# Output stores of four steps begun by ScalarE, in ScalarE's own DMA queue, instead of SyncE

## The chip, the cores and the metric

One core of a Trainium2 chip runs the kernel. The metric is the device time in microseconds (us) of one launch. The engines are named as in the profile: PE (TensorE, matmul), PEld (its weight loads), DVE (VectorE), ACT (ScalarE), POOL (GpSimd) and SP (SyncE). SP computes nothing here; it begins transfers. "ACTq" and "SPq" are the sequencers of ACT and SP: rows with that name issue transfers or wait.

## The reference

For each of 33280 tokens of 192 numbers, a convolution over the token and the six before it, with softmax weights that depend on token and head, and then a layer of 1024 hidden units:

```python
def _attn_ref(x, weight_gen):            # x (8, 4160, 192), weight_gen (8, 4160, 8, 7)
    w = softmax(weight_gen, axis=-1)     # over the 7 taps
    out = np.einsum('bshk,bskhg->bshg', w, x_unf)   # x_unf: the token and 6 before it
    return out.reshape(B, S, D)

def _moe_ref(x, w_in, w_out, g_ln):      # w_in (192, 1024), w_out (1024, 192)
    h = x @ w_in
    solu = h * softmax(h)
    ln = (solu - mean(solu)) / sqrt(var(solu) + 1e-6) * g_ln
    return ln @ w_out
```

## The kernel before

Each of the 128 partitions holds a run of 260 consecutive tokens. Step t (0 to 259) works on one token of each partition, so on 128 tokens. Inputs arrive in chunks of 16 steps (`load_x` in four parts, L87; `load_w`, L93). POOL multiplies taps and inputs for four steps at a time (L180) and adds part of the products (L195). From there a step runs like this:

- PE turns the step's inputs over (L477, two steps at a time). ACT copies the high half of them in 16 bits (`xhi`, L487), DVE the rest (`xld`, L491), and SP swaps halves between partitions with two small transfers (`sw`, L497).
- `mm1` (L511, L516): PE's first product, 128 x 1024, into one of three buffers `h`.
- `max` on DVE (L528), `exp` on ACT (L534), `solu` on DVE (L542), `sq` on ACT (L548): the softmax, its product with h, and the sums. Each is followed by a short read of the sum it collected.
- `hi` on ACT (L555) and `lo` on DVE (L559) write the result as two 16-bit halves into `hl` (three buffers).
- `tr` (L567): SP begins a transposing transfer hl to `hlT` (six buffers). An ACT `hi` that finds no free `hl` buffer waits until an earlier transposing transfer has landed.
- `mm2` (L607): PE's second product, 24 matmuls into `po`. There is one buffer `po`, so mm2 of the next step waits until `out` has read it.
- `out` (L618): ACT scales po into the step's place in `ot`, a tile of four steps with two buffers.
- `od` (L622): after every fourth `out`, the store of `ot` to memory, 384 KB. There are 66: 64 of four steps, one of three, one of the last step.

Every four steps there are also six small operations on the statistics, three of them on ACT (L582; L586 and L588; L594), and every 16 steps some on the input's norm (L145, L156 to L169) and the taps (L115, L120).

Each engine works its instructions off in the order in which the program was written. That order comes from a planner (`plan`, `issue_order`) that plays the whole program through with a table of costs and prints one list; the functions below are called in that list's order, so the place of an instruction among those of its engine is its place in the list. In the planner, `od` is a step of SP. Transfers begun by SP or ACT use eight semaphores in turn, in the order of the list, whichever engine begins them. A transfer waits, on the engine that begins it, until the transfer eight before it has landed.

Of the kernel before, what the change touches and what calls it, by code (L numbers as in the profile page):

```python
# [26 lines left out]
def tile_kernel(ctx: ExitStack, tc: tile.TileContext, x, weight_gen, w_in, w_out, g_ln, out):  # L27
    nc = tc.nc
# [10 lines left out]
    TG = 4  # L39
# [19 lines left out]
    o_run = out.rearrange("(p t) d -> p t d", t=RUN)  # L59
# [372 lines left out]
    o_of = {}  # L432
# [186 lines left out]

    def store(t):  # L620
        t0 = RUN - 1 if t == RUN - 1 else t - t % TG
        nc.sync.dma_start(o_run[:, t0 : t + 1, :], o_of[t // TG][:, t0 % TG : t % TG + 1, :])  # L622

    def at(op, *args):
        return lambda t: op(t, *args)
# [4 lines left out]
    def at_chunk(op, *args):  # L630
# [4 lines left out]
        xhi=high_x, xld=low_x, mm1=first_product,  # L635
        max=maximum, exp=exponentials, solu=solu, sq=squares, hi=high_half, lo=low_half,
        tr=transpose_s, mm2=second_product, out=finish, od=store, lw=at_chunk(load_w),
    )
    for n in range(2):
# [69 lines left out]
    t0=132.6, t0_0=11.9, t0_4=-51.5, t1=101, t1_0=56.2, t1_4=-6.3, t2=148.6, t2_0=60.2, t2_4=246.7,  # L709
# [335 lines left out]
```

## Time and profile before

| | |
|---|---|
| three runs | 1245.5, 1243.78, 1245.46 us, median 1245.46 |
| the profiled execution | 1243.28 us, its span 1241.5 us |
| busy share of the span | PE 96%, DVE 93%, POOL 92%, ACT 91% |
| granted TensorE clock | 0.996 over the span |
| transfers | 219.18 MB, most of them in packets under 512 B |
| stores (L622) | 64 of 384.0 KB, one of 288.0 KB, one of 96.0 KB; 3.4 us from issue to landing (median) |

The span runs from the first to the last instruction of the program; the 1.8 us between it and the execution's time lie around the program. A busy share is an average over the whole span. A wait is told with the engine and line that waited, what it waited for, and then microseconds in total, how often, and the longest. Waits of sequencers (SPq, ACTq) are not part of an engine's idle time. A transfer's row on SPq or ACTq lasts as long as the sequencer is busy beginning it, not until the data has landed.

### The profile page before, as it was taken

What the parts mean: (1) busy time and instruction counts of PE and PEld (TensorE: products, weight loads), DVE (VectorE), ACT (ScalarE), POOL (GpSimd) and SP (SyncE); (2) the same over time, 40 slices, a digit from 0 to 9 for tenths busy, and PEclk for the clock granted to TensorE, in tenths of its full rate; (3) what the DMA queues carried; (4) which work ended last, traced back from release to release, by engine and by line L of the source; (5) the groups of instructions that cost most, each with busy time, mean ns of one, the idle gap of its engine ahead of it and who ended that gap; (6) DMA issues with size and microseconds to landing.
All of it is one profiled execution on the core that took longest, in us unless ns stands there. A gap on an engine that the chain in (4) does not pass through costs nothing. (4 is left out here: it accounts for less than half of the span.)

```text
span 1241.5 us, 27360 instructions
## 1 busy us (share of the span) xinstructions
PE 1188.7 (96%) x10296; PEld 818.6 (66%) x10296; DVE 1151.7 (93%) x1777; ACT 1127.1 (91%) x2286; POOL 1140.1 (92%) x235
## 2 busy tenths in 40 slices
PE   1799999999999999999999999999999999999998
PEld 1467666666666676666666666666666666666766
DVE  6778989999899999999999999999999999999994
ACT  5789999899999989899998999999898999988895
POOL 5999999999999999999999999999999999999500
PEclk9899999999999999999999999999999999999999
DMA  7579797888988889898978989898988979887685
GB/s 246 106 158 223 139 217 158 182 177 182 194 161 203 166 190 181 178 206 144 219 154 192 185 177 207 158 204 171 184 178 176 216 149 200 159 156 138 137 166 125
DMA packets 585491, 219.18 MB, mean 177 GB/s; under 512 B 548623, under 2 KB 566031, under 8 KB 585102
## 3 DMA queue, kind: packets, MB, share of 16 engines
q1 hardware_dynamic: 585056, 216.32, 84.2%
q8 instruction: 81, 1.33, 0.4%
q10 hardware_dynamic: 302, 1.11, 0.3%
q14 instruction: 52, 0.43, 0.1%
HBM read 45.60 MB, written 25.56 MB: 57 GB/s over the span
## 5 line engine op out<-in xcount | busy, mean ns | idle before, releaser
L180 POOL TENSOR_TENSOR pr<-xt,wt 128x5376 f32<-128x5376 f32 (+1 forms) x67 | 631.2, 9420 | 0.2
L607 PE MATMUL po<-w_hl,hlT 128*128 128x192 f16 x6168 | 551.1, 246 | 6.9 <-ACT ot L618 6.9
L607 PEld LDWEIGHTS <-hlT 128*128 128x128 f16 x6240 | 522.8, 98 | 52.6 <-issue 10.6
L195 POOL TENSOR_TENSOR pr<-pr 128x2304 f32<-128x2304 f32 (+1 forms) x122 | 449.5, 3684 | 7.4
L559 DVE SCALAR_TENSOR_TENSOR hl<-h,hl 128x1024 f16<-128x1024 f32 x260 | 316.4, 1221 | 41.6 <-ACT hl L555 24.7
L542 DVE SCALAR_TENSOR_TENSOR h<-h,row,e 128x1024 f32<-128x1024 f32 x260 | 333.0, 1282 | 15.5 <-ACT e L534 14.4
L528 DVE TENSOR_SCALAR_CACHE_REDUCE h<-h,row 128x1024 f32<-128x1024 f32 x260 | 334.3, 1286 | 5.9 <-PE h L516 5.3
L555 ACT ACTIVATE hl<-h 128x1024 f16<-128x1024 f32 x260 | 266.7, 1027 | 41.2 <-DVE h L542 20.9
L534 ACT ACTIVATE e<-h,stats 128x1024 f32<-128x1024 f32 x260 | 291.8, 1122 | 8.8 <-DVE h L528 7.8
L548 ACT ACTIVATE e<-h,stats 128x1024 f32<-128x1024 f32 x260 | 290.7, 1118 | 3.2 <-DVE hl L559 2.7
L516 PEld LDWEIGHTS <-xh 128*128 128x128 f16 x1560 | 131.5, 98 | 234.2 <-issue 111.8
L516 PE MATMUL h<-w_odd,xh 128*128 128x512 f16 x780 | 190.9, 381 | 0.0
L516 PE MATMUL h<-wa_hi,xh 128*128 128x512 f16 x520 | 178.2, 384 | 0.0
L618 ACT ACTIVATE ot<-po,stats 128x192 f32<-128x192 f32 x257 | 110.2, 429 | 29.9 <-PE po L607 29.8
L511 PE MATMUL h<-w_odd,turned 64*128 64x512 f16 x390 | 106.2, 379 | 5.8 <-DVE hl L559 4.6
L511 PE MATMUL h<-wb_hi,xh 64*128 64x512 f16 x260 | 99.5, 383 | 7.4 <-DVE hl L559 7.2
L511 PE MATMUL h<-w_odd,xh 64*128 64x512 f16 x390 | 106.3, 380 | 0.0
L477 PE MATMUL pa<-ident,pr 128*128 128x128 f32 x738 | 95.3, 277 | 7.7 <-POOL pr L180 3.9
L511 PE MATMUL h<-wb_hi,turned 64*128 64x512 f16 x260 | 99.6, 383 | 0.0
L477 PEld LDWEIGHTS pa<-ident,pr 128*128 128x128 f32 x738 | 86.2, 143 | 19.9 <-POOL pr L180 5.6
L516 PE MATMUL h<-wa_lo,xh 128*128 128x512 f16 x260 | 99.1, 381 | 0.0
L511 PEld LDWEIGHTS <-xh 64*128 64x128 f16 x780 | 53.7, 94 | 47.1 <-issue 22.6
(90 smaller groups left out, 995.8 us busy)
## 6 DMA issues: line engine op xcount, KB each, us to landing
out_dram<-ot SPq DMA_DIRECT2D x64, 384.0 KB, 3.4
xt<-in_x_dram SPq DMA_DIRECT2D x30, 576.0 KB, 4.7
xt<-in_x_dram SPq DMA_DIRECT2D x30, 480.0 KB, 4.3
turned<-xh SPq DMA_DIRECT2D x260, 32.0 KB, 2.2
wt<-in_weight_gen_dram SPq DMA_DIRECT2D x16, 448.0 KB, 5.4
hlT<-hl SPq DMA_TRANSPOSE x260, 4.9
xt<-in_x_dram SPq DMA_DIRECT2D x1, 1536.0 KB, 10.7
pr<-in_moe_w_out_dram SPq DMA_DIRECT2D x1, 1024.0 KB, 7.9
```

The costliest lines, as they stand in the source:

```text
L180: nc.gpsimd.tensor_tensor(out=window(pr, 0, [(ROW, K), (HG, n * H), (1, HG)]), in0=window(xt, t * D, [(D, K), (HG, n * H), (1, HG)]), in1= ...
L195: nc.gpsimd.tensor_tensor(out=b, in0=b, in1=a, op=ALU.add)
L477: nc.tensor.matmul(pa[:, k], source[:, first : first + P], ident, is_transpose=True, start=at == 0, stop=at == 3 * len(sources) - 1,)
L511: nc.tensor.matmul(h[:, fs], last[(f + odd) % 2][rows, low], rhs[rows], start=n == 0, stop=False)
L516: nc.tensor.matmul(h[:, fs], xh[:, 2 * odd, low], rhs[:, fs], start=False, stop=n == 2)
L528: nc.vector.tensor_scalar(h, h, row(t, BACK), 3.0e38, op0=ALU.mult, op1=ALU.min, accum_out=stat(t, NMAX))
L534: nc.scalar.activation(e, h_of[t], AF.Exp, bias=stat(t, NMAX), scale=-1.0, accum_out=stat(t, Z))
L542: nc.vector.scalar_tensor_tensor(out=h, in0=h, scalar=row(t, SCALE), in1=e, op0=ALU.mult, op1=ALU.mult, accum_out=stat(t, M))
L548: nc.scalar.activation(e_of.pop(t), h_of[t], AF.Square, bias=stat(t, M), scale=-float(FF), accum_out=stat(t, Q),)
L555: nc.scalar.activation(hl[:, 0, :], h_of[t], AF.Copy, scale=2.0**14)
L559: nc.vector.scalar_tensor_tensor(out=hl[:, 1, :], in0=h_of[t], scalar=2.0**14, in1=hl[:, 0, :], op0=ALU.mult, op1=ALU.subtract,)
L607: nc.tensor.matmul(po[:, :D], hlT[:, half * NJ + j, :], w2_hl[:, j, w, :], start=n == 0, stop=n == len(terms) - 1,)
```

## The change

The store calls ACT's queue instead of SP's. The planner still counts `od` as a step of SP, so the list, and with it the order of all other instructions on every engine, stays what it was: the 66 stores leave SP's stream and stand in ACT's, each at its place in the list.

```diff
     def store(t):
         t0 = RUN - 1 if t == RUN - 1 else t - t % TG
-        nc.sync.dma_start(o_run[:, t0 : t + 1, :], o_of[t // TG][:, t0 % TG : t % TG + 1, :])
+        nc.scalar.dma_start(o_run[:, t0 : t + 1, :], o_of[t // TG][:, t0 % TG : t % TG + 1, :])
```

The first place is the store of the tile ot_7630, at about 606 us of the profiled execution. In ACT's stream before, the fourth `out` of the tile (L618, ot_7630) is followed at once by `sq` (L548):

```order
L555 ACTIVATE hl_7807<-h_7684 128x1024
L534 ACTIVATE e_7811,stats_135<-h_7741,stats_135 128x1024
L618 ACTIVATE ot_7630<-po_7777,stats_135 128x192
L548 ACTIVATE e_7756,stats_135<-h_7684,stats_135 128x1024
L145 ACTIVATE junk_7860,squares_x_116<-xt_7636 128x768
L555 ACTIVATE hl_7862<-h_7741 128x1024
L618 ACTIVATE ot_7878<-po_7834,stats_135 128x192
```

And now, with the store right between them:

```order
L555 ACTIVATE hl_7807<-h_7684 128x1024
L534 ACTIVATE e_7811,stats_135<-h_7741,stats_135 128x1024
L618 ACTIVATE ot_7630<-po_7777,stats_135 128x192
L622 DMA out_0_dram<-ot_7630 128x768
L548 ACTIVATE e_7756,stats_135<-h_7684,stats_135 128x1024
L145 ACTIVATE junk_7860,squares_x_116<-xt_7636 128x768
L555 ACTIVATE hl_7862<-h_7741 128x1024
L618 ACTIVATE ot_7878<-po_7834,stats_135 128x192
```

The store now stands ahead of `sq` and of all that ACT does after it.

In SP's stream the same store stood before between parts of an input load and two transposing transfers:

```order
L497 DMA turned_7736<-xh_7698 64x256 x2
L87 DMA xt_7636<-in_x_dram 128x960
L567 DMA_TRANSPOSE hlT_7761<-hl_7739 128x16x128
L87 DMA xt_7636<-in_x_dram 128x1152
L622 DMA out_0_dram<-ot_7630 128x768
L567 DMA_TRANSPOSE hlT_7832<-hl_7807 128x16x128
L567 DMA_TRANSPOSE hlT_7883<-hl_7862 128x16x128
L497 DMA turned_7887<-xh_7804 64x256 x2
```

Now the transposing transfer of hl_7807 follows the load directly; the store no longer stands ahead of it, and nothing else moved.

The next store, of ot_7878 (about 625 us), stands in ACT's stream behind two small operations of the statistics:

```order
L618 ACTIVATE ot_7878<-po_8012,stats_135 128x192
L586 ACTIVATE stats_135<-stats_135 128x4
L588 ACTIVATE stats_135<-stats_135 128x4x2
L622 DMA out_0_dram<-ot_7878 128x768
L534 ACTIVATE e_8062,stats_135<-h_7991,stats_135 128x1024
L145 ACTIVATE junk_8094,squares_x_116<-xt_7636 128x768
```

Here `exp` (L534) is the next that comes behind the store. Of the 66 stores, ten follow their `out` directly; the others have one or two of ACT's instructions between: L586 and L588 (13), L487 (14), L582 (6), L162 and L163 (6), L594 (2), or a long one, L534, L548 or L555 (15).

## The prediction

> **What bounds the kernel now.** I read the page's busy shares first, then the busy time of each engine in stretches of the steady part, then the list of waits, then the timeline around two stores.
>
> ```profile
> span 1241.5 us, 27360 instructions
> PE 1188.7 (96%) x10296; PEld 818.6 (66%) x10296; DVE 1151.7 (93%) x1777; ACT 1127.1 (91%) x2286; POOL 1140.1 (92%) x235
> ...
> 500.00:700.00 200.00, 197.76 (x1729) 135.56 (x1727) 191.93 (x291) 186.79 (x376) 198.59 (x40) 1.00 0.90 186
> 700.00:900.00 200.00, 199.12 (x1734) 135.86 (x1732) 194.97 (x302) 188.51 (x383) 197.20 (x40) 1.00 0.89 181
> 900.00:1100.00 200.00, 199.00 (x1738) 136.61 (x1737) 193.21 (x297) 188.72 (x386) 197.63 (x40) 1.00 0.89 178
> ```
>
> The columns of the stretches are, after the length, the busy time of PE, PEld, DVE, ACT and POOL, then clock, DMA share and GB/s. PE is busy for 197.8 to 199.1 of 200 us at the full clock: in the steady part it sets the pace. Everything else is close behind. ACT has 11.3 to 13.2 us idle in 200, which at a store every 18.5 us (about 11 in 200) is 1.0 to 1.2 us for each store. What PE can still win there is 1 to 2 us in 200, some 10 us over the kernel; what it can lose has no such limit.
>
> ```profile
> ACT ot L618 <- PE po L607: 29.8, 28, 1.9
> PE po L607 <- ACT ot L618: 6.9, 13, 1.7
> PE h L511 <- DVE hl L559: 11.7, 13, 5.4
> ACT hl L555 <- DMA hlT<-hl: 6.1, 8, 1.7
> ```
>
> So PE waits for ACT in one place directly: mm2 cannot start before `out` has emptied the only `po`. And the whole cost of late transposing transfers to ACT is 6.1 us in 8 waits. mm2 does not appear in the list as waiting for one.
>
> SP, the queue that loses the stores, around 605 us:
>
> ```profile
> 599.98 0.58 SPq L87 DMA_DIRECT2D xt<-in_x_dram  x1
> 600.67 3.45 SPq L567 DMA_TRANSPOSE hlT<-hl  x1
> 604.22 1.17 SPq L497 DMA_DIRECT2D turned<-xh  x2
> 605.43 1.39 SPq L87 DMA_DIRECT2D xt<-in_x_dram  x1
> 606.94 3.33 SPq L567 DMA_TRANSPOSE hlT<-hl  x1
> 610.31 0.57 SPq L87 DMA_DIRECT2D xt<-in_x_dram  x1
> 610.98 0.38 SPq L622 DMA_DIRECT2D out_dram<-ot  x1
> 611.47 6.64 SPq L567 DMA_TRANSPOSE hlT<-hl  x2
> ...
> 618.19 1.02 ACT L555 ACTIVATE hl<-h 128x1024 f16<-128x1024 f32 x1 [0.98 <-DMA hlT<-hl]
> 619.25 1.22 DVE L559 SCALAR_TENSOR_TENSOR hl<-h,hl 128x1024 f16<-128x1024 f32 x1 [1.64 <-ACT hl L555]
> 620.67 2.14 PE L607 MATMUL po<-w_hl,hlT 128*128 128x192 f16 x24 [0.42 <-ACT ot L618]
> ```
>
> SP runs almost without a gap (about 0.1 us between transfers), most of it in transposing transfers of 2 to 3.5 us. The three last rows show where that lateness ends: `hi` waits 0.98 us, `lo` 1.64, and mm2 0.42.
>
> **What is removed from SP.** Each store and the gap behind it leave SP: 0.38 + 0.1 us here.
>
> ```profile
> L622 SPq DMA_DIRECT2D out_dram<-ot x66: 333/531/1332, 86.9 to 1238.5; - x66
> ```
>
> At the median it is 0.53 + 0.1, times 66 some 42 us of SP's time. It is worth only what late transfers cost. The bound is the 6.1 us of the third wait above passing whole into PE; in the example 0.42 of 0.98 us passed, which makes 2.6 us of 6.1; and the store's 0.48 us is half of the 0.98. I take a gain of 2 us, with 0 and 6.1 as the ends.
>
> **What is added to ACT.** Each store has three parts: the wait for its `out`, the time in which ACT's sequencer begins the transfer, and the return to the next instruction. The wait for the transfer eight places before costs nothing: seven before the store at 610.98 is the load at 599.98, so the eighth was begun over 5.9 us before this store's `out` is done (605.90 by the rows further down), and transposing transfers land 4.9 us after their issue at the median:
>
> ```profile
> DMA to landing us min/median/max: 4.2/4.9/8.4
> ```
>
> If a transfer is late there, all of ACT stands behind it; the cover is that distance.
>
> How long ACT's sequencer is held the trace does not show for this place. The nearest rows are SP's own stores and the first transfers of the kernel, where ACT and SP begin transfers side by side:
>
> ```profile
> 0.71 0.40 ACTq L205 DMA_DIRECT2D hlT<-in_moe_w_in_dram  x1
> 0.72 0.40 SPq L93 DMA_DIRECT2D wt<-in_weight_gen_dram  x1
> 1.15 1.16 ACTq L77 DMA_DIRECT2D xt<-in_x_dram  x2
> ...
> 294.54 2.37 SPq L567 DMA_TRANSPOSE hlT<-hl  x1
> 299.12 0.35 SPq L622 DMA_DIRECT2D out_dram<-ot  x1
> ...
> 624.05 1.93 SPq L567 DMA_TRANSPOSE hlT<-hl  x1
> 626.09 0.93 SPq L622 DMA_DIRECT2D out_dram<-ot  x1
> ```
>
> A store that finds SP idle takes 0.35 us (18 of them, 0.33 to 0.35). One right behind a transposing transfer takes longer: 31 of them, 0.53 to 1.33, median 0.89. So something that both use is still at work when SP's sequencer is through with the transposing transfer. ACT's transfers took 0.40 and 0.58 us beside SP's. For ACT's stores I take 0.54 where SP is not in a transposing transfer, and 0.89 where it is. Comparing the end of each of the 66 `out` rows with SP's rows, SP is in one at 37 of them, with 1.32 us still to go on average.
>
> Now what of this ACT feels. The two places:
>
> ```profile
> 605.47 0.43 ACT L618 ACTIVATE ot<-po,stats 128x192 f32<-128x192 f32 x1
> 606.32 1.12 ACT L548 ACTIVATE e<-h,stats 128x1024 f32<-128x1024 f32 x1 [0.42 <-DVE hl L559]
> 606.70 2.14 PE L607 MATMUL po<-w_hl,hlT 128*128 128x192 f16 x24
> 609.16 0.42 ACT L618 ACTIVATE ot<-po,stats 128x192 f32<-128x192 f32 x1
> 611.82 2.15 PE L607 MATMUL po<-w_hl,hlT 128*128 128x192 f16 x24
> ...
> 624.23 0.42 ACT L618 ACTIVATE ot<-po,stats 128x192 f32<-128x192 f32 x1
> 624.54 0.22 ACT L586 ACTIVATE stats<-stats 128x4 f32<-128x4 f32 x1
> 624.78 0.22 ACT L588 ACTIVATE stats<-stats 128x8 f32<-128x8 f32 x1
> 624.90 1.10 ACT L534 ACTIVATE e<-h,stats 128x1024 f32<-128x1024 f32 x1
> ```
>
> At the first, `out` ends at 605.90. ACT idled until 606.32 anyhow, so a store of 0.54 us with 0.12 for the two hand-overs (SP's gap between transfers) delays `sq` by 0.66 - 0.42 = 0.24 us. At the second, `out` ends at 624.65 and `exp` starts at 624.90: L586 and L588 cover 0.25, and 0.41 is left, provided that ACT's sequencer can begin a transfer while ACT still computes. Where a long instruction (1.1 us) stands between, nothing is left. Read so at all places, the delays are: ten directly behind `out`, 0.41 us each on average; 13 behind L586 and L588, 0.42; 6 behind L582, 0.56; 6 behind L162 and L163, 0.34; 14 behind L487, 0.18; 2 behind L594, 0.24; 15 behind a long one, 0. That is 4.1 + 5.5 + 3.4 + 2.0 + 2.5 + 0.5 = 18 us of ACT's time. With 0.35 us for every store it is 10, with 1.33 it is 58, and with the mixture I take (0.54 and 0.89) 28 us.
>
> Most of it is taken up before PE sees it. The next `out` after 605.90 ends at 609.58 and its mm2 starts at 611.82: 2.2 us of slack. After the `out` that ended at 605.90 itself it was 606.70 - 605.90 = 0.8. I carried each of the 66 delays down ACT's rows, took off the idle time in front of them, and charged PE with what is over the slack of the next `out`. An estimate, then: 0.1 us in all at 0.35 per store, 1.2 at 0.54, 6.7 for the mixture, 23 at 1.33 everywhere, 19 with 1.33 only beside transposing transfers. The same delay reaches DVE through `exp` and `hi`, and PE through the buffers `h`, where it waits 11.7 us now, one wait of 5.4 among them; I add 2 us for that (ends 0 and 6).
>
> The end of the kernel costs nothing either way: the last store is begun by whichever queue after the last `out`, and takes 0.33 us.
>
> **The sum**, against the profiled execution's 1243.28 us (1.8 of it around the span): + 6.7 + 2 - 2 = 1250.0. The median of the runs stands 2.2 us higher than that execution; I put the forecast between the two sums, at 1251. A measurement of this kernel tells about 0.2%, 2.5 us, from no change; this is 0.4%.
>
> **The rivals.**
> - The gain of SP is the larger part: ACT's stores take 0.35 to 0.40, as in its row at 0.71, and are covered, and SP's transposing transfers come earlier. ACT then costs 0.1 to 1 us and SP gives up to 6.1: 1239 to 1243 beside the median. For it: SP's rows stand end to end, and mm2 did wait 0.42 us at 620.67 after a chain that began there. Against it: only 8 waits for transposing transfers in the whole kernel. It decides if the gain exceeds 2.5 us, so if more than 40% of those 6.1 us were PE's. 22%.
> - Nothing that can be told from no change: 1.2 + 1 - 2, so within 2.5 us of 1245.5. It takes 0.54 us or less beside transposing transfers also. 23%.
> - ACT's queue cannot begin a transfer while SP's is beginning one. At the 37 places ACT's store then waits out SP's 1.32 us and starts after it. With 0.54 behind that, ACT feels 63 us and PE 40; with 0.89, 76 and 50, by the same carrying down. That is more than ACT's 1.0 to 1.2 us of idle per store at these places, and the time is 1283 to 1296. For it: the 0.93 us at 626.09 behind a transposing transfer. Against it: at 0.71 and 0.72 both sequencers are at it together and both take 0.40. 15%.
>
> The last of these is also the account of the Trainium skill. Its page Perfetto Trace Analysis, section DMA Instruction — HWDGE, says that a transfer's row holds a wait for a lock, that the descriptor generator is then locked for exclusive use, and that it is freed when all descriptors are made. By that rule the sum would be the one just given; the two rows of 0.40 us side by side do not agree with a lock over the whole row, but no transposing transfer is among them.
>
> **Chances and range.** The forecast, slower by 0.2 to 1.6%: 40%; with the queues that exclude each other, slower in all: 55%. Same 23%, faster 22%. The range leaves out the last rival (15%) and little at the low end: from 1239 (the whole gain) to 1275 (1.33 us at every store, 23 us, and 6 through DVE, on the median). The forecast's own range is 1248 to 1266.
>
> **What would show it.** Stores on ACTq: their duration, median near 0.54 and near 0.9 beside transposing transfers; over 1.5 there speaks for the last rival, 0.35 to 0.40 the covered case. ACT's idle before the instruction behind each store should be put down to the issue. PE's waits for L618 should grow from 6.9 us to about 13, and ACT's for hlT shrink from 6.1 to about 3. It would be wrong if ACT's sequencer cannot run ahead of the engine: then all 66 stores cost their full time, 35 us and more, whatever stands in front.

## The result, and the profile after

The kernel with ACT's stores took 1253.72 us (median of three runs), the one before 1245.32: 1.0066 of its time, 95% interval 1.0049 to 1.0082, or 8.2 us slower by that ratio. A second measurement gave 1254.0 us and 1.0063 (1.0045 to 1.0081). A fourth run of the first measurement, the profiled one, had a TensorE clock of 0.56 of full speed and took 2033.52 us, so it is not counted and the profile shown here is from the second measurement, at the same clock as that of before (0.997 and 0.996).

The page of the profile after, its first rows and the queues:

```profile
span 1251.7 us, 27310 instructions
PE 1191.7 (95%) x10296; PEld 818.8 (65%) x10296; DVE 1153.3 (92%) x1777; ACT 1132.2 (90%) x2286; POOL 1140.5 (91%) x235
...
q1 hardware_dynamic: 575552, 190.75, 78.6%
q10 hardware_dynamic: 9806, 26.67, 6.4%
```

The stores' 25.6 MB have left SP's queue (q1) for ACT's (q10). Every engine has as many instructions as before and is busy for 0.2 to 5.1 us more; every one also stands idle longer, PE by 7.2 us. The waits that answer to those shown before, and ACT's new ones:

```profile
ACT ot L618 <- PE po L607: 25.5, 27, 1.8
...
PE h L511 <- DVE hl L559: 15.8, 21, 5.4
...
PE po L607 <- ACT ot L618: 9.4, 14, 1.9
ACT hl L555 <- DMA hlT<-hl: 9.1, 9, 1.7
...
ACT e L534 <- issue: 2.3, 13, 0.2
...
ACT e L548 <- issue: 1.1, 6, 0.2
```

PE waits 4.1 us more for `lo` (11.7 before) and 2.5 more for `out` (6.9 before). ACT waits 3.0 us more for transposing transfers to free `hl` (6.1 before), where the forecast had 3 us less. The stores in the view of the tile ot, and then the landing of the transposing transfers (L567):

```profile
L622 ACTq DMA_DIRECT2D out_dram<-ot x66: 338/338/377, 82.4 to 1248.8; - x66
DMA to landing us min/median/max: 1.6/4.2/7.8
...
DMA to landing us min/median/max: 4.3/5.1/9.3
```

Each store holds ACT's sequencer for 0.338 us (median), at most 0.377; 39 of the 66 began while SP's sequencer was in a transposing transfer. The stores land after 4.2 us (3.4 before), the transposing transfers after 5.1 (4.9 before). At the places of the prediction, the stores of ot_7630 and ot_7878:

```profile
609.95 0.43 ACT L618 ACTIVATE ot<-po,stats 128x192 f32<-128x192 f32 x1
610.41 0.34 ACTq L622 DMA_DIRECT2D out_dram<-ot  x1
610.81 1.11 ACT L548 ACTIVATE e<-h,stats 128x1024 f32<-128x1024 f32 x1 [0.42 <-DVE hl L559]
...
627.39 0.43 ACT L618 ACTIVATE ot<-po,stats 128x192 f32<-128x192 f32 x1
627.70 0.22 ACT L586 ACTIVATE stats<-stats 128x4 f32<-128x4 f32 x1
627.95 0.22 ACT L588 ACTIVATE stats<-stats 128x8 f32<-128x8 f32 x1
627.96 0.35 ACTq L622 DMA_DIRECT2D out_dram<-ot  x1
628.36 1.11 ACT L534 ACTIVATE e<-h,stats 128x1024 f32<-128x1024 f32 x1 [0.19 <-issue]
```

The store begins 0.03 us after its `out`. At the first place the idle time of 0.42 us that was there before covers it whole. At the second it begins while L588 runs and leaves 0.19 us of idle ("issue": the engine waited for nothing else). So ACT's sequencer does begin transfers while ACT computes.

### The profile page after: what moved, and what is told of

It reads as the page before. It is cut to its first block, busy times and chain, and to the rows that moved or that the text cites. A ratio compares the mean times of both kernels' runs of the same rounds, so it can differ in the third digit from the quotient of the medians.

```text
span 2031.7 us, 27310 instructions
## 1 busy us (share of the span) xinstructions
PE 1995.1 (98%) x10296; PEld 1150.7 (57%) x10296; DVE 1189.2 (59%) x1777; ACT 1164.9 (57%) x2286; POOL 1140.0 (56%) x235
## 3 DMA queue, kind: packets, MB, share of 16 engines
q8 instruction: 81, 1.33, 0.3%
## 4 chain that ended last, share of the span: by engine, by line
PE 98%; POOL 1%; DMA 0%; issue 0%; DVE 0%; ACT 0%; ACTq 0%; POOLq 0%; DVEq 0%
PE po L607 44%; PE h L516 30%; PE h L511 15%; PE pa L477 8%; PE h L607 1%; DMA xt<-in_x_dram 0%; POOL pr L180 0%; PE po L374 0%; DVE hl L559 0%; POOL xt L239 0%; ACT ot L618 0%; POOL wt L111 0%; DVE h L528 0%; PE po L396 0%; ACT hl L555 0%
## 5 line engine op out<-in xcount | busy, mean ns | idle before, releaser
L607 PE MATMUL po<-w_hl,hlT 128*128 128x192 f16 x6168 | 939.8, 341 | 1.5 <-ACT ot L618 1.5
L607 PEld LDWEIGHTS <-hlT 128*128 128x128 f16 x6240 | 765.1, 132 | 226.9 <-issue 90.4
L534 ACT ACTIVATE e<-h,stats 128x1024 f32<-128x1024 f32 x260 | 289.2, 1112 | 140.1 <-DVE h L528 137.2
L618 ACT ACTIVATE ot<-po,stats 128x192 f32<-128x192 f32 x257 | 108.3, 421 | 449.3 <-PE po L607 446.9
L516 PE MATMUL h<-w_odd,xh 128*128 128x512 f16 x780 | 311.5, 563 | 0.0
L548 ACT ACTIVATE e<-h,stats 128x1024 f32<-128x1024 f32 x260 | 288.9, 1111 | 4.8 <-ACT ot L618 1.8
L555 ACT ACTIVATE hl<-h 128x1024 f16<-128x1024 f32 x260 | 265.2, 1021 | 12.0 <-DVE h L542 5.6
L516 PE MATMUL h<-wa_hi,xh 128*128 128x512 f16 x520 | 263.2, 551 | 0.0
L487 ACT CAST xh<-pa 128x384 f16<-128x384 f32 x130 | 62.3, 479 | 229.7 <-PE pa L477 228.6
L511 PE MATMUL h<-w_odd,xh 64*128 64x512 f16 x390 | 161.5, 546 | 0.0
L477 PE MATMUL pa<-ident,pr 128*128 128x128 f32 x738 | 156.5, 392 | 5.1 <-POOL pr L180 3.9
L511 PE MATMUL h<-w_odd,turned 64*128 64x512 f16 x390 | 160.3, 544 | 0.0
L516 PE MATMUL h<-wa_lo,xh 128*128 128x512 f16 x260 | 153.3, 590 | 0.0
L511 PE MATMUL h<-wb_hi,xh 64*128 64x512 f16 x260 | 136.9, 526 | 6.7 <-DVE hl L559 6.7
```

The lines of the kernel that those rows point to most:

```text
L477: nc.tensor.matmul(pa[:, k], source[:, first : first + P], ident, is_transpose=True, start=at == 0, stop=at == 3 * len(sources) - 1,)
L511: nc.tensor.matmul(h[:, fs], last[(f + odd) % 2][rows, low], rhs[rows], start=n == 0, stop=False)
L516: nc.tensor.matmul(h[:, fs], xh[:, 2 * odd, low], rhs[:, fs], start=False, stop=n == 2)
L534: nc.scalar.activation(e, h_of[t], AF.Exp, bias=stat(t, NMAX), scale=-1.0, accum_out=stat(t, Z))
L548: nc.scalar.activation(e_of.pop(t), h_of[t], AF.Square, bias=stat(t, M), scale=-float(FF), accum_out=stat(t, Q),)
L555: nc.scalar.activation(hl[:, 0, :], h_of[t], AF.Copy, scale=2.0**14)
```

## The experiments

Two theories stood at the start. A: ACT is held at each store, and what it does next reaches PE late. B: the stores' packets, now in a queue of their own beside SP's, make the transposing transfers land later, and `hi` waits for these. All ratios are to the kernel before, in runs on the same chip, and differences in us are worked out from the ratios. Waits come from one trace of each kernel, while executions of the kernel before range from 1241.9 to 1250.8 us, so a difference of 2 or 3 us between the waits of two traces is no firm figure.

**The change again**, unchanged.

> The changed kernel once more, for its time and a trace at the full clock. Theory A (ACT is held at each store, and its late out and hi reach PE): 1252 to 1256 us; ACT's idle before the instruction behind the stores sums to 15 to 30 us, PE's wait for L618 grows from 6.9 us to about 13, transposing transfers land no later than 4.9 us after their issue. Theory B (the stores' packets now run beside the transposing transfers from a second queue and make them land later): the same time, but the landing goes above 5.2 us at the median, and ACT's wait for hlT above 6.1 us.

1254.0 us, 1.0063 (1.0045 to 1.0081). ACT's idle before the instructions behind the stores sums to 18.9 us, as A has it, but the kernel before idles 12.6 us in front of the same instructions, so the stores added 6.3. Both predictions of the trace came in part: PE's waits grew as A has it, though for `out` to 9.4 us and not to 13, and ACT's wait for hlT grew to 9.1 as B has it, while the median landing went to 5.1 us, short of B's 5.2. The median hides where it happens. Of the transposing transfers between 60 and 1160 us, I set those in flight together with a store apart from the rest: before, 112 land after 5.33 us on average, the others after 5.01. With the change, 110 beside a store take 6.15, the others 4.94. It is not that long transfers are the likelier to have a store beside them: of these 110, the 109 that lie in the same stretch in all the traces take 5.06 us without stores and 5.31 before.

**No stores.** In `store` of the kernel before:

```diff
-        nc.sync.dma_start(o_run[...], o_of[t // TG][...])
+        if t >= RUN - 2:
+            nc.sync.dma_start(o_run[...], o_of[t // TG][...])
```

> Before, but without the 64 stores of four steps (only the last two, of steps 256 to 259, remain; 63 or 64 tiles of results are left in the chip). It tells what SP's and the transfers' relief is worth with no cost on ACT. Theory A: 0 to 3 us faster than before, since late transposing transfers cost ACT only 6.1 us. Theory B: stores cost by their packets, so 3 us or more faster.

1238.07 us, 0.9931 (0.9912 to 0.995), 8.6 us faster. That is more than A allowed. Its waits:

```profile
PE h L511 <- DVE hl L559: 10.2, 11, 5.4
PE po L607 <- ACT ot L618: 4.3, 9, 1.7
...
ACT hl L555 <- DMA hlT<-hl: 0.2, 1, 0.2
```

The wait for hlT is all but gone, and PE's for `out` fell by 2.6 us. So the stores cost 8.6 us already before the change, and the change made that about 16.

**The stores behind a long instruction.** On the changed kernel, the call of each store is put off in the list until after the next `exp` or `sq`:

```diff
-    for op, t in issue_order(...):
-        ops[op](t)
+    for op, t in issue_order(...):
+        if op == "od" and t < RUN - 6:
+            held_back.append(t)
+            continue
+        ops[op](t)
+        if op in ("exp", "sq") and held_back:
+            ops["od"](held_back.pop())
```

> The stores in ACT's queue, but each held back until after the next exp or sq of ACT (1.1 us), so that the transfer is begun while ACT computes. Theory A: ACT's delay is covered, and the time falls to 1243 to 1247 us. Theory B: still 1251 to 1255, since packets and queue are as in the change.

1258.37 us, 1.0088 (1.0062 to 1.0114): no cure. The hold itself was covered, since behind all stores but one (and the last two) ACT's next instruction followed without idle; behind that one it idled 0.9 us. The waits are those of B:

```profile
PE po L607 <- ACT ot L618: 17.0, 22, 2.6
ACT hl L555 <- DMA hlT<-hl: 16.3, 13, 3.1
...
PE h L511 <- DVE hl L559: 12.8, 16, 5.4
```

ACT waits 16.3 us for hlT, PE 17.0 for `out`, and hardly more than before for `lo`. The transposing transfers beside a store take 6.21 us to land, the others 4.91. So the stores in ACT's queue, with ACT hardly held, cost 11 us here, SP's relief already taken off. The size is not firm: the six executions took 1250.8 to 1261.1 us, and three of them, the traced one among them, had a granted clock of 0.992 or 0.993. Its trace has two stretches of 3 us at half of the clock, worth 3 us at most.

**ACT's part alone.** On the kernel before, with its stores on SP, ACT begins a transfer of 512 bytes at the same places:

```diff
+        if t < RUN - 2:
+            nc.scalar.dma_start(spare, o_of[t // TG][:, t % TG, :1])
         nc.sync.dma_start(o_run[...], o_of[t // TG][...])
```

> All stores as before in SP's queue, and besides at the same 64 places a transfer of 512 bytes (128 x 1 numbers of ot into a spare tile) begun by ACT, with the store's wait for its out. It adds ACT's part of the change alone. Theory A: 1252 to 1257 us, the change's loss without SP's gain. Theory B: within 2.5 us of before, since hardly any bytes move.

1257.88 us, 1.0099 (1.0078 to 1.012): A holds too. The transfer holds ACT's sequencer for 0.472 us, longer than the store's 0.338, so this is above what the change takes of ACT. The same with no stores beside it:

```diff
-        nc.sync.dma_start(o_run[...], o_of[t // TG][...])
+        if t < RUN - 2:
+            nc.scalar.dma_start(spare, o_of[t // TG][:, t % TG, :1])
+        else:
+            nc.sync.dma_start(o_run[...], o_of[t // TG][...])
```

> No stores of four steps at all (as in no_stores, 1238 us), but ACT begins the 64 transfers of 512 bytes, each with the wait for its out. It is ACT's part with SP free of stores. Theory A (ACT's hold of 0.34 to 0.47 us per store reaches PE): 1246 to 1251 us, the same 8 to 13 us that these transfers cost beside the stores. Theory B (the loss is in transposing transfers that land later beside a store from a second queue): within 2.5 us of no_stores.

1248.39 us, 1.0017 (1.0006 to 1.0028), against 0.9931 with no stores: 1.0017 - 0.9931 is 0.86%, 10.7 us for the hold alone (about 3 us either way by the two intervals). Its waits show the road (the lines of the code have moved by one, so L512 is mm1's L511, L549 `sq`, L556 `hi`, L560 `lo`, L608 mm2, L619 `out`):

```profile
PE h L512 <- DVE hl L560: 14.8, 20, 5.5
...
PE po L608 <- ACT ot L619: 4.3, 6, 2.0
...
PE h L512 <- ACT e L549: 1.9, 6, 1.0
...
ACT hl L556 <- DMA hlT<-hl: 1.6, 6, 0.5
```

PE waits 4.6 us more for `lo`, 1.6 more for `sq` (L549 here; 0.3 without the transfers), and not more for `out`. A's mark is the wait for `lo`: over the traces of the table further down it is 14.8 to 16.3 us where ACT is held and 10.2 to 13.7 where it is not. The change has this mark (15.8), and a longer wait for `out` (9.4) besides.

**The same 512 bytes behind a long instruction**, put off as the stores were, with SP's stores in place (63 of them):

```diff
         ops[op](t)
+        if op == "od" and t < RUN - 6:
+            held_back.append(t)
+        elif op in ("exp", "sq") and held_back:
+            last = held_back.pop()
+            nc.scalar.dma_start(spare, o_of[last // TG][:, last % TG, :1])
```

> Stores as before on SP, and the 64 transfers of 512 bytes on ACT, held back until after the next exp or sq, so that ACT computes while its sequencer begins them. Theory A: the hold is covered, 1244 to 1248 us, against 1258 for the same transfers right behind their place. Theory B says the same, and then the loss of the stores held back in the same way (1258 us) is by their bytes alone. If it is 1254 or more, covering is no cure and that conclusion falls.

1247.29 us, 1.0007 (0.9992 to 1.0023). Covering does cure the hold. So what the stores cost when they were covered in the same way is no hold. The waits of this run warn of another reading:

```profile
PE h L512 <- DVE hl L560: 13.2, 17, 5.4
...
ACT hl L556 <- DMA hlT<-hl: 9.8, 12, 1.9
PE po L608 <- ACT ot L619: 9.6, 15, 1.7
```

ACT's wait for hlT and PE's for `out` are as long as with the change, without its loss and with hardly any bytes in ACT's queue. So these two waits alone don't show B. What shows it are the times, and how long the transposing transfers take.

**A constant instead of ot**, same places, 512 bytes:

```diff
+        if t < RUN - 2:
+            nc.scalar.dma_start(spare, inside)
```

> Stores as before on SP, and at the same 64 places the transfers of 512 bytes on ACT, but of a constant, so that they don't wait for the out. If the wait for out is what exposes the hold: the transfer is begun while out computes, and 1245 to 1250 us; if a transfer on ACT's sequencer costs as such: 1254 to 1259 us.

1254.28 us, 1.0067 (1.0047 to 1.0086): two thirds of the 0.99% remain without the wait for `out`. In its trace the transfers behind L586 and L588 still begin only in the last 0.2 us of L588, and ACT idles 0.3 us behind them: ACT's sequencer was not further ahead than that. Behind `out`, where they now begin before its end, ACT does not idle. So the wait for `out` exposes a part of the hold only.

**Half of the bytes.** On the changed kernel, each store of four steps takes the last two only:

```diff
+        if t < RUN - 2:
+            t0 = t - 1
         nc.scalar.dma_start(o_run[...], o_of[t // TG][...])
```

> The change, but each of the 64 stores by ACT takes only the last two of its four steps (half of the bytes, at the same place, with the same wait for out; half of the results are left out). ACT's hold is as in the change. If the bytes on a second queue are the rest of the loss: half way between 1248 (512 bytes, no stores) and 1254 (the change), so 1250 to 1252 us, with transposing transfers beside a store landing about 5.6 us after their issue in place of 6.15. If the loss is the hold alone: 1253 to 1255 us.

1246.96 us, 1.0002 (0.9991 to 1.0012), faster than expected.

```profile
PE h L511 <- DVE hl L559: 16.0, 20, 7.2
...
PE po L607 <- ACT ot L618: 5.1, 6, 1.9
...
ACT hl L555 <- DMA hlT<-hl: 3.3, 6, 1.2
```

With the same hold (0.338 us at the median) and the same wait for `lo`, leaving out half of the bytes takes away the whole 8 us of the change. Transposing transfers beside a store land after 5.74 us, between 5.33 and 6.15, and ACT's wait for hlT is 3.3 us. Some of this is that fewer bytes move at all: no run stores half of the bytes from SP's queue, so how much is not shown.

**SP's stores, further back in SP's queue.** On the kernel before, each store is put off until behind the next one, two or four transposing transfers of the list:

```diff
+        if op == "od" and t < RUN - 6:
+            held_back.append([t, 2])          # or 1, or 4
+            continue
         ops[op](t)
+        if op == "tr" and held_back:
+            held_back[0][1] -= 1
+            if not held_back[0][1]:
+                ops["od"](held_back.pop(0)[0])
```

> Stores on SP, each held back behind the next two transposing transfers, ACT as before. If what the stores cost before (8 us by no_stores) is that they stand ahead of transposing transfers in SP's queue: 1239 to 1243 us. If it is their bytes: within 2.5 us of before.

> Stores on SP, each held back behind the next one transposing transfer. If what counts is the transposing transfer right behind the store: as with two, 1238 to 1241 us. If each transfer passed counts: about 1242 us.

> Stores on SP, each held back behind the next four transposing transfers. If a store costs wherever SP is behind, and none of its places is free: 1239 to 1245 us. If passing transposing transfers goes on to gain: 1237 to 1239 us, near the kernel without stores.

Two later: 1239.18 us, 0.9948 (0.9932 to 0.9964), faster than both kernels. One later: 1250.43 us, 1.0029 (1.0015 to 1.0044), slower than before. Four later: 1434 us, since there are two buffers `ot` and the `out` of two groups on must wait for the store (one tile is left unstored at the end). Its main waits are:

```profile
ACT ot L618 <- DMA out_dram<-ot: 190.8, 54, 7.3
PE po L607 <- ACT ot L618: 134.0, 68, 4.8
```

So place in SP's queue decides most of what the stores cost: 6.5 us of the 8.6 are had back with every byte still moved. With two later, ACT's wait for hlT is 2.9 us, and transposing transfers beside a store land after 5.13 us instead of 5.33. But it is not a matter of passing transposing transfers one by one, as the expectation for one later had it: that one loses, with a wait for hlT of 6.3 us, as before. Why one place is worse and the next one better stays open.

**All runs side by side.** Two sums from the traces say more than the waits do. The first adds up the 260 rows of L567 on SPq, the time in which SP's sequencer is busy beginning transposing transfers. The second is ACT's idle time in front of the instruction right behind each transfer of ACT, less what the kernel before idles in front of the same instructions.

| kernel | time | rows of L567, us | ACT's added idle, us |
|---|---|---|---|
| no stores | 0.9931 | 628 | - |
| SP's stores two later | 0.9948 | 654 | - |
| before | 1 | 686 | - |
| SP's stores one later | 1.0029 | 688 | - |
| 512 bytes, no stores | 1.0017 | 630 | 12.1 |
| 512 bytes behind a long instruction | 1.0007 | 690 | 0 |
| 512 bytes of a constant | 1.0067 | 689 | 7.5 |
| 512 bytes | 1.0099 | 684 | 12.4 |
| half of the bytes | 1.0002 | 678 | 6.3 |
| the change | 1.0063 | 721 | 6.3 |
| ACT's stores behind a long instruction | 1.0088 | 732 | 0.9 |

With 512 bytes the rows stay as they were, and the time grows by about as much as ACT's added idle: by 12.3 us for 12.4, by 8.3 for 7.5, by 0.9 for none, and by 10.7 for 12.1 without stores. By that measure, which is an estimate, the change's own hold is worth about 6 us. The stores lengthen the rows wherever they are begun, and most from ACT's queue. The two sums are no formula: half of the bytes comes out faster than they would have it, and one later slower.

## Why the prediction was right, and where its steps were not

The direction, the forecast of 1251 us (measured 1254) and the range held. That is luck more than working: with the hold that was measured, the forecast's own parts are 0.1 + 2 - 2, no change, and stores of 0.35 to 0.40 us were the sign that it had named for its covered case, the rival in which the kernel gets faster. A hold taken too long, a road to PE taken too short, a gain that did not come and bytes that were not counted came to about the right sum.

- How long ACT is held. Forecast 0.54 us, and 0.89 beside a transposing transfer of SP, from SP's own stores. Measured 0.338, beside SP's transposing transfers and away from them (0.377 at most). What lengthens a store behind a transposing transfer in SP's stream (0.53 to 1.33 us) does not hold ACT's sequencer. The lower row, 0.35 for a store that finds SP idle, was the right neighbour.
- That ACT's sequencer begins a transfer while ACT computes: right. Behind a long instruction nothing is left, and behind L586 and L588 0.17 to 0.21 us, which is the forecast's working with 0.34 in place of 0.54: 0.34 + 0.12 - 0.25 = 0.21.
- What of the hold reaches PE: this is the step that failed, at "charging PE with what is over the slack of the next `out`". For 0.35 us it gave 0.1 us through `out` and 2 us through DVE. Measured 10.7 us for a hold of 0.47 with no stores, with the growth in PE's listed waits on `lo` (4.6 us) and `sq` (1.6), none on `out`. `sq`, `hi` and `lo` free the buffers h, and the forecast had no row by row account of that road. By the table, nearly all of what ACT idles more ends up in the time. Six of the nine microseconds by which the span grew from no_stores can be found as idle of PE between 60 and 1160 us (8.8 against 14.5); where the rest arose is open.
- SP's gain: forecast 2 us, at most 6.1 (the wait for hlT, which stands fourth in its list and not third). Without the stores it is 8.6, though there their bytes are gone too, and 6.5 by two places in the queue. The bound took only waits that the profile puts down to a transfer. The time taken off SP was too small as well: it counted the stores' own rows, some 42 us, while the stores also lengthen the rows of the transposing transfers, by 57 us before (628.5 to 685.9).
- The bytes in a second queue were not in the sum. The forecast let the transposing transfers start earlier and land as before; they land 0.8 us later beside a store, and their rows take 35 us more of SP (686 to 721), most of the 42 us that the stores freed. So the gain of SP did not come: ACT's wait for hlT rose to 9.1 instead of falling to 3. The changed kernel against the one without stores is 1.0063 / 0.9931, 1.3%, 16.5 us. With half of the bytes and the same hold it is 8.8, so the hold is at most that and the bytes at least 7.7. The exact split is open, since the runs don't add up to it: by the covered stores the bytes alone would be more than the whole.

The rivals. Queues that exclude each other: as that rival had it, with ACT held meanwhile, it is refuted by 39 stores of 0.34 us begun within SP's transposing transfers. The Trainium skill (Perfetto Trace Analysis, section DMA Instruction — HWDGE) counts the wait for the lock into a transfer's row; in these 39 rows there is none. Whether the transfer waits somewhere else is not settled: the 39 land after 4.89 us on average, the other 27 after 3.39, and of the 512 bytes without stores the 33 begun within a transposing transfer land after 3.84, the other 31 after 2.42. Against a lock over a whole row of SP's, two of the 39 had landed before the row in which they began was over.

The eight semaphores in turn are no cause either: in the trace of the change, no store began, and no transfer behind a store, earlier than 0.97 us after the transfer eight before it had landed.

SP's gain as the larger part: it is larger than that rival had it, but it comes only as long as the stores stay out of a second queue. At the place shown in the prediction both sides can be seen. The transposing transfer begun right beside the store now takes 3.92 us of SP's sequencer (3.33 before), the next two together 5.86 (6.64), and the wait of 0.98 us of `hi` is gone.

```profile
611.07 3.92 SPq L567 DMA_TRANSPOSE hlT<-hl  x1
615.04 0.58 SPq L87 DMA_DIRECT2D xt<-in_x_dram  x1
615.73 5.86 SPq L567 DMA_TRANSPOSE hlT<-hl  x2
...
621.69 1.02 ACT L555 ACTIVATE hl<-h 128x1024 f16<-128x1024 f32 x1
622.75 1.23 DVE L559 SCALAR_TENSOR_TENSOR hl<-h,hl 128x1024 f16<-128x1024 f32 x1 [0.66 <-ACT hl L555]
624.42 2.14 PE L607 MATMUL po<-w_hl,hlT 128*128 128x192 f16 x24
```

## What to carry to other kernels

A transfer moved to another engine's queue does not only free its old queue and hold the new engine; its packets can now run beside those it used to stand in line with, so compare the rows and the landing of the transfers beside it, apart from the others, before and after. A short hold on an engine that works to the beat of the bound one can cost more than the slack of the next direct handover shows, so follow every buffer that its later instructions free, or begin the transfer behind a long instruction: here that took the cost of the 512 bytes from 0.99% to nothing that can be told from noise, though it did not help the stores, whose bytes are the other part. Before changing the queue of a transfer that nobody waits for, try other places in the queue that it has: here two places later was worth 0.5%, and one place later lost 0.3%.

## What the runs showed of the hardware that was not expected

ACT's sequencer takes 0.338 us to begin a store of 384 KB, the same within SP's transposing transfers and outside them, and 0.472 us for 512 bytes of 128 partitions into the chip's own memory. Where ACT has to wait for it, its next instruction starts 0.05 us after the row ends. The sequencer is not far ahead of the engine: with two instructions of 0.22 us in front, a transfer that waits for none of them begins only 0.2 us before the second one ends. A store in flight lengthens the time for which SP's sequencer is busy beginning a transposing transfer: the same 109 of them take 2.50 us on average with no stores, 2.89 with the stores begun by SP, 3.22 with the stores begun by ACT, and 2.55 with 512 bytes begun by ACT and no stores.
